# Weight signs on ScalarE, weight differences on GpSimd, and a new order of all engines, in a recurrent attention and feed-forward kernel

## The chip, the core and the metric

The kernel runs on one core of a Trainium2 chip. The time is device microseconds of one execution of the whole program, and the median of several runs is given. A profile of one execution stands beside it. The engines are TensorE (PE; its weight loads are PEld), VectorE (DVE), ScalarE (ACT), GpSimd (POOL) and SyncE (SP), which issues every DMA.

## The reference

```python
q, k, v, alpha: (4, 8, 768, 48)         # batch, heads, positions, head size
for t in range(S):                      # S = 768
    state = alpha[:, :, t, :, None] * state + einsum('bhd,bhe->bhde', k[:, :, t], v[:, :, t])
    y[:, :, t] = einsum('bhd,bhde->bhe', q[:, :, t], state)
x = y.transpose(0, 2, 1, 3).reshape(3072, 384)
h = x @ w_in                            # (384, 2048)
g = h * clip(h + 3, 0, 6) / 6
out = g @ w_out                         # (2048, 384)
```

The two weights come to the kernel as 64-bit floats, everything else as 32-bit floats.

## The kernel before

**Tiles.** The 3072 tokens are 24 chunks of 128 (j = 0 to 23), six to a batch. Two chunks are a group (g = 0 to 11). A chunk goes through the recurrence in blocked form and gives 128 columns of x; a group goes through the feed-forward part.

**Recurrence, chunk j.** `la`, `lk`, `lq`, `lv` load alpha, k, q, v. For j under 6, `ta`, `tk`, `tq` transpose on TensorE into one of four PSUM banks and `ca` copies alpha out on ScalarE; from j = 6 on, these transposes are stream transposes of VectorE (line 286) out of tiles `aq`, `kq`, `qq`, two of each. Those tiles have a strip of padding that GpSimd sets to one with a memset (line 257) when a tile is first used (j = 6 and 7). `r` and `p` are the two decay scans on VectorE (lines 309 and 320), `k` and `q` scale k and q (line 332), `sc` and `m` are scores and mask, `qa` copies q beside the masked scores (ScalarE), `kb`/`ck` (or `kt`, `kw`, `kr` through DRAM) turn k round, `u` is the state update on TensorE, `sm` adds it up on VectorE (`sm.j.0` the half state), `st` decays it on GpSimd (line 409), `sv` places it (ScalarE), `ya` and `yb` are the output of both half blocks, `cy` copies it into x (ScalarE).

**Weights.** They come in 16 slices of 128x768 64-bit words (`w.i`, 768 KB each): 0 to 7 are `w_in`, 8 to 15 `w_out`. A slice lands in one of three raw buffers (two more lie in the tile of hidden values). `d1` rounds the low words and `d2` takes the magnitude of the high words (ScalarE), `d3` clips and shifts them (VectorE), `d4` adds the low words (GpSimd, line 217). The sign has two forms. In the usual form the third instruction of `d3`, a mask and an or (line 210), puts the sign bits back. For the slices in `BY_HALVES` the step `dx` (`sign`, ScalarE, line 191) writes the sign into the low words instead, and `d3` has two instructions (lines 203 and 205).

**Feed-forward.** Groups 0 and 1 use plain products, `f.g.i` (`fa` and `fb` a chunk at a time) with relu `fr` (ScalarE) and product `fg` (VectorE), and chunks 0 and 1 use `b` for the second weight, with the copy `bo` and the store `so`. From group 2 on, the first weight is used in 20 fast products `M.g.i` of sums of x (`xc`) and sums of weights (`y`, 25 of them, VectorE, made once); `n` copies products out (ScalarE), `o` combines them (VectorE), `e` and `h` are relu and product. From group 1 on, the second weight is used in seven fast products `P.g.i` of 128x192 outputs. They need sums of hidden values (`s`, VectorE) and four differences of the weight's quarters, `x.0` to `x.3`, each 128x1536, made once: `x.0` and `x.2` are read by P.g.4 and P.g.2, `x.1` by P.g.3, `x.3` by P.g.6; `x.1` overwrites a quarter that `b.1.0`, `b.1.1`, `b.0.0` and `b.0.1` read. `K` copies partial outputs (ScalarE), `G.g.i` finishes an output quarter (VectorE; `G.g.3` a copy on ScalarE), `O.g.i` stores it.

**Order.** Nothing is scheduled at run time. A string of 1788 words is the program's order: each word is a step and its numbers (`fa.2.0` is weight slice 2 into bank 0), and each engine does its own steps in the order of the string, waiting by semaphore for what a step reads. `z.m.n` are n matmuls of the identity with no use for their result. SyncE's queue is in the same order: a DMA that waits holds up those behind it. In before, the differences are VectorE's:

```python
    def minus(out, in0, in1):
        nc.vector.tensor_tensor(out=out, in0=in0, in1=in1, op=ALU.subtract)

    def combine_w2(i):
        minus(*[(t[3], b[1, 1], b[0, 1]), (t[1], b[0, 1], b[0, 0]), (t[2], b[1, 1], t[1]),
                (t[4], b[1, 0], t[2])][i])
```

Of the kernel before, what the change touches and what calls it, by code (L numbers as in the profile page):

```python
# [17 lines left out]
def kernel(  # L18
# [32 lines left out]
    nc = tc.nc  # L51
# [124 lines left out]
    BY_HALVES = {0, 1, 2, 4}  # L176
# [573 lines left out]
    with tc.manual_schedule():  # L750
        run("""z.0.5 z.0.3 z.0.1 z.0.8 qa.0.0 w.0 d2.0 d3.0 la.0 ta.0.0 ca.0 r.0 lk.0 tk.0.1 k.0
               z.0.2 p.0 la.1 ta.1.2 lq.0 tq.0.3 ca.1 r.1 lk.1 lv.0.0 sv.0.0 d1.0 kb.0.0 ck.0 z.0.2
               u.0.2.1 sm.0.0 sv.0.1 q.0 qa.0.1 tk.1.0 k.1 p.1 z.0.2 sc.0.2.3 m.0 la.2 ta.2.0 ca.2
               dx.0 w.2 d2.2 kb.1.0 ck.1 lq.1 r.2 sm.0.1 st.1 tq.1.2 q.1 d3.2 z.0.3 d1.2 dx.2 lv.1.1
               u.1.3.1 sv.1.0 sm.1.0 p.2 sm.1.1 sc.1.0.2 m.1 ya.0.3 yb.0 cy.0 lq.2 w.1 d1.1 tq.2.1
               q.2 d4.2 lk.2 tk.2.3 k.2 fa.2.0 d4.0 st.2 sc.2.0.2 d2.1 d3.1 m.2 dx.1 d4.1 qa.1.1
               lk.3 la.3 ta.3.1 ca.3 la.4 fa.0.1 sv.1.1 w.3 r.3 ta.4.3 ca.4 r.4 tk.3.1 k.3 kb.2.0
               qa.1.0 d2.3 ya.1.2 yb.1 cy.1 fa.1.2 lq.3 ck.2 d1.3 p.3 d3.3 lv.2.2 u.2.3.2 sm.2.0
               d4.3 fb.2 tq.3.1 q.3 fb.1 qa.2.0 sm.2.1 sv.2.0 st.3 fr.0.2.0 fg.0.2 lk.4 tk.4.0
               sv.2.1 w.5 d2.5 k.4 d3.5 d1.5 qa.3.0 d4.5 qa.2.1 sc.3.1.3 m.3 w.6 d2.6 d1.6 d3.6 d4.6  # L760
               lv.3.0 lq.4 w.7 kb.3.2 fb.0 f.0.3.3 kb.4.0 ya.2.1 ck.3 u.3.3.2 sm.3.0 fr.0.3.1 fg.0.3
               fr.0.1.0 fg.0.1 qa.3.1 sv.3.0 sm.3.1 p.4 d2.7 sv.3.1 d1.7 d3.7 d4.7 f.0.5.0 fr.0.5.1
               fr.0.0.0 fg.0.5 fg.0.0 tq.4.3 ck.4 la.5 ta.5.2 f.0.6.3 ca.5 w.4 d2.4 ya.3.0 yb.3 cy.3
               fr.0.6.1 yb.2 cy.2 w.9 d2.9 q.4 qa.4.1 d1.4 d1.9 dx.4 la.6 w.8 d3.4 r.5 lk.5 w.10
               d3.9 p.5 ca.6 fg.0.6 d4.9 w.12 lq.5 lv.4.1 d2.8 d3.8 f.0.7.2 d1.8 st.4 d4.8 d4.4 w.11
               fr.0.7.0 fg.0.7 f.1.7.0 fr.1.7.1 fg.1.7 sc.4.0.2 m.4 f.1.1.1 fr.1.1.0 fg.1.1 f.1.3.3
               fr.1.3.1 d2.10 d1.10 tk.5.3 f.1.0.2 d2.12 d3.10 d4.10 w.13 fg.1.3 fr.1.0.0 fg.1.0 k.5
               d3.12 lq.6 f.1.6.0 f.1.2.1 u.4.1.0 sm.4.0 d1.12 d4.12 sv.4.0 qa.4.0 ya.4.2 fr.1.6.1
               fg.1.6 w.15 tq.5.3 fa.4.3 sv.4.1 d2.11 kb.5.1 d2.13 fr.1.2.0 f.1.4.2 fr.1.4.1 d1.11
               sm.4.1 q.5 r.6 d3.11 d3.13 fg.1.4 d4.11 lv.5.0 lk.6 tq.6 p.6 d2.15 d3.15 fg.1.2 d1.13  # L770
               d4.13 sc.5.0.3 yb.4 f.1.5.0 fr.1.5.1 fg.1.5 tk.6 m.5 b.1.0.2 fb.4 b.1.1 d1.15 d4.15
               st.5 y.5 w.14 la.7 lk.7 cy.4 d2.14 qa.5.1 ck.5 b.0.0.1 fr.0.4.0 d3.14 k.6 q.6 ca.7
               fg.0.4 d1.14 d4.14 x.0 y.1 y.10 b.0.1 y.0 y.2 u.5.2 P.1.0.0 K.1.0 qa.5.0 sv.5.0
# [159 lines left out]
```

## Time and profile before

| | us |
|---|---|
| median of 3 runs | 536.4 (536.31 to 536.47) |
| the profiled execution's own time | 536.33 |
| its span, first to last instruction | 534.5 |
| TensorE busy | 524.2 |
| VectorE busy | 477.1 |
| ScalarE busy | 257.6 |
| GpSimd busy | 50.4 |
| `d3` third instruction (line 210), mean of one | 0.96 |
| sign on ScalarE (line 191), mean of one | 1.94 |
| a difference of 128x1536 on VectorE (line 647) | 1.74 to 1.75 |

The page's busy times are of one execution, and a matmul counts as busy until its modelled end, so neighbours overlap. A row of the groups gives line, engine, operation, written and read tiles with their shapes and the count, then the group's busy time and the mean of one in ns, then the engine's idle time just before them and who ended it. A row of the timeline gives start, length, engine, line and operation, and in brackets the idle time before it and its releaser. A row of the chain of work that ended last gives start, length, engine, tile, line and count.

Busy time counts a tail that overlaps the next instruction. Where an engine is never idle, a step costs the distance from its start to the next start, and this is shorter: 1.35 us for the two instructions of `d3` in the halves form and 2.09 for the three of the usual form, 1.67 for a sign, 1.67 for a difference on VectorE, 1.54 for a mask step, 1.34 for `r`, 1.14 for `p`, 0.6 for `q`, `y` and most other steps of 128x512.

### The profile page before, as it was taken

The page shows a single profiled execution, that of the slowest core. Times are in us where ns is not written, and L with a number is a line of the kernel's source. Part 1 is how long each engine was busy: PE and PEld are TensorE (multiplying, and loading weights), DVE is VectorE, ACT ScalarE, POOL GpSimd, SP SyncE. Part 2 cuts the span into 40 slices and gives each one's busy share as a digit, 9 for nine tenths or more (in the row PEclk, how much of TensorE's full clock was granted, in tenths as well). Part 3 has the DMA queues.
Part 4 walks back from the last instruction along what each step waited for, and adds up shares of the span by engine and source line. Part 5 has one row for each costly group of instructions (what it writes and reads, how often), then busy time and mean ns, then how long its engine had stood idle before and what let it go on. Part 6 is the DMA issues. An engine that isn't in the chain of part 4 may idle for free.

```text
span 534.5 us, 15145 instructions
## 1 busy us (share of the span) xinstructions
PE 524.2 (98%) x6306; PEld 498.9 (93%) x6306; DVE 477.1 (89%) x849; ACT 257.6 (48%) x503; POOL 50.4 (9%) x71
## 2 busy tenths in 40 slices
PE   7799999999999999999999999999999999999997
PEld 7698886789999999999999999999999999999996
DVE  6999989999999899998999999999999898586381
ACT  3889864212653553543644434642633544553330
POOL 5333435100000000000010000000000000000000
PEclk9999999999999999999999999999999999999999
DMA  9998877006615155254354455055364042100001
GB/s 174 215 255 256 208 220 164 7 2 158 149 32 121 28 132 130 50 136 101 82 109 113 95 124 139 20 129 122 81 144 97 18 97 48 36 3 1 29 1 44
DMA packets 124100, 54.40 MB, mean 102 GB/s; under 512 B 83328, under 2 KB 116864, under 8 KB 124032
## 3 DMA queue, kind: packets, MB, share of 16 engines
q1 hardware_dynamic: 124032, 53.44, 43.0%
q8 instruction: 49, 0.80, 0.7%
q14 instruction: 19, 0.16, 0.1%
HBM read 44.50 MB, written 8.91 MB: 100 GB/s over the span
## 4 chain that ended last, share of the span: by engine, by line
PE 88%; DVE 6%; POOL 2%; ACT 1%; DMA 1%; issue 0%; SPq 0%; DVEq 0%; POOLq 0%
PE m_ps L703 34%; PE m_ps L600 34%; PE m_ps L478 6%; PE t_ps L455 4%; PE t_ps L346 2%; PE t_ps L429 2%; PE m_ps L489 2%; DMA v<-in_v_dram 1%; PE m_ps L516 1%; DVE rings L647 1%; PE t_ps L282 1%; DVE raw L537 1%; ACT raw L191 1%; DVE g_sb L647 1%; DVE w L537 1%; POOL v L96 1%
## 5 line engine op out<-in xcount | busy, mean ns | idle before, releaser
L606 ACT COPY g_sb<-m_ps 128x512 f32<-128x512 f32 x110 | 63.7, 584 | 124.1 <-PE m_ps L600 101.3
L703 PE MATMUL m_ps<-w,g_sb 128*128 128x192 f32 x704 | 121.7, 327 | 0.0
L703 PEld LDWEIGHTS m_ps<-w,g_sb 128*128 128x128 f32 x704 | 113.7, 190 | 0.4
L703 PE MATMUL m_ps<-rings,g_sb 128*128 128x192 f32 x528 | 91.5, 326 | 0.0
L703 PEld LDWEIGHTS m_ps<-rings,g_sb 128*128 128x128 f32 x528 | 85.4, 190 | 0.1
L600 PE MATMUL m_ps<-xc,w 128*128 128x128 f32 x640 | 82.7, 277 | 0.3 <-DVE w L541 0.3
L600 PEld LDWEIGHTS m_ps<-xc,w 128*128 128x128 f32 x640 | 77.5, 192 | 1.5 <-issue 0.5
L494 ACT ACTIVATE r<-g_sb,half 128x512 f32<-128x512 f32 x80 | 57.0, 722 | 31.5 <-DVE g_sb L541 12.4
L498 DVE SCALAR_TENSOR_TENSOR g_sb<-r,g_sb 128x512 f32<-128x512 f32 x80 | 53.7, 682 | 6.8 <-ACT r L494 5.4
L600 PE MATMUL m_ps<-xT,raw 128*128 128x128 f32 x400 | 52.5, 277 | 0.0
L600 PEld LDWEIGHTS m_ps<-xT,raw 128*128 128x128 f32 x400 | 48.6, 192 | 0.6
L409 POOL TENSOR_TENSOR st<-sm,R 128x192 f32<-128x192 f32 x20 | 12.9, 643 | 353.7 <-DVE sm L439 295.7
L647 DVE TENSOR_TENSOR g_sb<-g_sb 128x512 f32<-128x512 f32 (+1 forms) x55 | 42.1, 793 | 1.3 <-PE m_ps L703 1.1
L600 PE MATMUL m_ps<-xT,w 128*128 128x128 f32 x320 | 42.0, 276 | 0.0
L600 PEld LDWEIGHTS m_ps<-xT,w 128*128 128x128 f32 x320 | 39.3, 192 | 0.1
L366 ACT COPY A<-q 48x256 f32<-48x256 f32 x88 | 35.5, 404 | 5.0 <-DVE q L332 3.7
L356 DVE TENSOR_TENSOR A<-t_ps,mask 64x256 f32<-64x256 f32 x96 | 36.0, 413 | 0.4
L478 PE MATMUL m_ps<-xT,w 128*128 128x256 f32 x144 | 32.8, 382 | 0.0
L600 PE MATMUL m_ps<-xc,raw 128*128 128x128 f32 x240 | 31.8, 276 | 0.0
L478 PEld LDWEIGHTS m_ps<-xT,w 128*128 128x128 f32 x144 | 26.7, 190 | 3.6
L309 DVE TENSOR_TENSOR_SCAN R<-t,ones 128x516 f32<-128x516 f32 x24 | 29.6, 1233 | 0.5 <-ACT t L300 0.4
L600 PEld LDWEIGHTS m_ps<-xc,raw 128*128 128x128 f32 x240 | 29.6, 192 | 0.1
(104 smaller groups left out, 730.3 us busy)
## 6 DMA issues: line engine op xcount, KB each, us to landing
raw<-in_moe_w_out_dram SPq DMA_DIRECT2D x8, 768.0 KB, 5.3
raw<-in_moe_w_in_dram SPq DMA_DIRECT2D x6, 768.0 KB, 7.1
v<-in_v_dram SPq DMA_DIRECT2D x48, 96.0 KB, 3.0
out_dram<-oh SPq DMA_DIRECT2D x44, 96.0 KB, 1.7
far<-kq SPq DMA_DIRECT2D x64, 64.0 KB, 2.2
kb<-far SPq DMA_DIRECT2D x64, 64.0 KB, 2.1
aq<-in_alpha_dram SPq DMA_DIRECT2D x36, 96.0 KB, 2.4
qq<-in_q_dram SPq DMA_DIRECT2D x36, 96.0 KB, 2.5
```

The source lines that it names most:

```text
L309: nc.vector.tensor_tensor_scan(out=reverse(R, n - 1, n), data0=reverse(ax, n, n), data1=reverse(ones, n, n), initial=0.0, op0=ALU.mult, op ...
L356: nc.vector.tensor_tensor(out=to[:, a], in0=sc[a][half], in1=mask[half, half].unsqueeze(1).to_broadcast([HB, NP, HB]), op=ALU.mult)
L366: nc.scalar.copy(out=to[:, a], in_=Q_t[j][64 * a : 64 * a + D, :, half])
L409: nc.gpsimd.tensor_tensor(out=st, in0=sm, in1=R_t[j][:, :, 0:1].to_broadcast([C, NP, D]), op=ALU.mult)
L455: nc.tensor.matmul(y_of(j, (i + 1) // 2, p)[:, HB * b : HB * b + HB], vb[:, p, e : e + 32], A_t[j][:, b, 2 * p + a], start=(b == 0 and i = ...
L478: nc.tensor.matmul(h[:, f], w1[:, kk, o : o + C], xT_t[g][:, kk], start=(kk == 0), stop=(kk == KT - 1))
L494: nc.scalar.activation(out=to, in_=h, func=AF.Relu, bias=half, scale=1.0 / 6.0)
L498: nc.vector.scalar_tensor_tensor(out=to, in0=r, scalar=1.0, in1=h, op0=ALU.min, op1=ALU.mult)
L600: nc.tensor.matmul(acc[g][i][:, f * C : (f + 1) * C], spots[w][:, f * C : (f + 1) * C], x_of(g, x), start=(first and f == 0), stop=last, s ...
L606: nc.scalar.copy(out=slots[z], in_=acc[g][i])
L647: nc.vector.tensor_tensor(out=out, in0=in0, in1=in1, op=ALU.subtract)
L703: nc.tensor.matmul(to[g], a, rhs[:, f], start=(first and f == 0), stop=(last and f == HF - 1), skip_group_check=True)
```

## The change

The second weight's slices 8 to 15 take the halves form: eight more `dx` steps on ScalarE, and for these slices two instructions of `d3` in place of three. The four differences `x` go from VectorE to GpSimd. The string is a new one of 1796 words; the steps are otherwise the same, and TensorE does the same 6306 instructions. The line numbers behind the differences move by three (L647 for GpSimd's differences becomes L650).

```diff
-    BY_HALVES = {0, 1, 2, 4}
+    BY_HALVES = {0, 1, 2, 4, *range(8, 16)}
...
+    def less(out, in0, in1):
+        nc.gpsimd.tensor_tensor(out=out, in0=in0, in1=in1, op=ALU.subtract)
+
     def combine_w2(i):
-        minus(*[(t[3], b[1, 1], b[0, 1]), (t[1], b[0, 1], b[0, 0]), (t[2], b[1, 1], t[1]),
+        less(*[(t[3], b[1, 1], b[0, 1]), (t[1], b[0, 1], b[0, 0]), (t[2], b[1, 1], t[1]),
                 (t[4], b[1, 0], t[2])][i])
...
-  run("""z.0.5 z.0.3 z.0.1 z.0.8 qa.0.0 w.0 d2.0 d3.0 la.0 ta.0.0 ca.0 r.0 lk.0 tk.0.1 k.0
-      z.0.2 p.0 la.1 ta.1.2 lq.0 tq.0.3 ca.1 r.1 lk.1 lv.0.0 sv.0.0 d1.0 kb.0.0 ck.0 z.0.2
-      u.0.2.1 sm.0.0 sv.0.1 q.0 qa.0.1 tk.1.0 k.1 p.1 z.0.2 sc.0.2.3 m.0 la.2 ta.2.0 ca.2
-      dx.0 w.2 d2.2 kb.1.0 ck.1 lq.1 r.2 sm.0.1 st.1 tq.1.2 q.1 d3.2 z.0.3 d1.2 dx.2 lv.1.1
-      u.1.3.1 sv.1.0 sm.1.0 p.2 sm.1.1 sc.1.0.2 m.1 ya.0.3 yb.0 cy.0 lq.2 w.1 d1.1 tq.2.1
-      q.2 d4.2 lk.2 tk.2.3 k.2 fa.2.0 d4.0 st.2 sc.2.0.2 d2.1 d3.1 m.2 dx.1 d4.1 qa.1.1
-      lk.3 la.3 ta.3.1 ca.3 la.4 fa.0.1 sv.1.1 w.3 r.3 ta.4.3 ca.4 r.4 tk.3.1 k.3 kb.2.0
-      qa.1.0 d2.3 ya.1.2 yb.1 cy.1 fa.1.2 lq.3 ck.2 d1.3 p.3 d3.3 lv.2.2 u.2.3.2 sm.2.0
-      d4.3 fb.2 tq.3.1 q.3 fb.1 qa.2.0 sm.2.1 sv.2.0 st.3 fr.0.2.0 fg.0.2 lk.4 tk.4.0
-      sv.2.1 w.5 d2.5 k.4 d3.5 d1.5 qa.3.0 d4.5 qa.2.1 sc.3.1.3 m.3 w.6 d2.6 d1.6 d3.6 d4.6
-      lv.3.0 lq.4 w.7 kb.3.2 fb.0 f.0.3.3 kb.4.0 ya.2.1 ck.3 u.3.3.2 sm.3.0 fr.0.3.1 fg.0.3
...
-      st.5 y.5 w.14 la.7 lk.7 cy.4 d2.14 qa.5.1 ck.5 b.0.0.1 fr.0.4.0 d3.14 k.6 q.6 ca.7
-      fg.0.4 d1.14 d4.14 x.0 y.1 y.10 b.0.1 y.0 y.2 u.5.2 P.1.0.0 K.1.0 qa.5.0 sv.5.0
-      qa.6.1 P.1.1.3 b.0.2 b.1.2 kb.6.0 ya.5.3 y.6 s.1.0.0 sm.5.0 sv.5.1 G.1.0.0 tk.7
-      s.1.1.1 s.1.2.3 x.1 yb.5 cy.5 b.1.3 sc.6.1.2 lv.6.2 ck.6 u.6.3.0 s.1.3.2 x.2 P.1.2
-      b.0.3 K.1.1 y.7 s.1.4 s.1.5 y.11 y.3 r.7 xc.2.1 x.3 y.4 y.8 xc.2.3 k.7 xc.2.0 xc.2.4
-      y.9 y.12 y.16 y.13 y.15 P.1.3.3 K.1.2 P.1.4 bo.1 P.1.5 xc.2.5 G.1.1.1 P.1.6 y.14 y.17
-      y.19 xc.2.6 sm.6.0 G.1.2.2 y.20 M.2.0.2 lv.12.1 la.8 O.1.1 O.1.0 ca.8 y.18 y.21 y.23
...
-      s.11.1.14 s.11.3.10 P.11.3.2 K.11.0 s.11.2.11 o.11.2.1 o.11.3.1 P.11.2 K.11.2
-      e.11.2.0 h.11.2 s.11.4 e.11.3.1 h.11.3 P.11.1.0 s.11.5 G.11.0.1 O.11.0 O.10.3 K.11.1
-      P.11.4 G.11.1.2 P.11.5 G.11.2.1 O.11.2 P.11.6 G.11.3.0 O.11.3 O.9.2 O.11.1""")
+  run("""z.0.3 z.0.2 z.0.8 qa.0.0 w.0 d2.0 d1.0 la.0 ta.0.0 ca.0 z.0.2 lk.0 tk.0.1 d3.0 r.0
+      k.0 p.0 dx.0 la.1 ta.1.2 ca.1 r.1 kb.0.3 ck.0 lq.0 z.0.2 tq.0.0 lv.0.0 u.0.1.2 sm.0.0
+      sv.0.1 z.0.5 q.0 qa.0.1 sc.0.1.3 sm.0.1 p.1 m.0 w.2 d2.2 z.0.3 lk.1 tk.1.0 k.1 lq.1
+      d1.2 dx.2 tq.1.2 q.1 z.0.1 kb.1.1 sc.1.0.3 d3.2 m.1 qa.1.0 ck.1 w.1 d2.1 d3.1 la.2
+      sv.0.0 ya.0.2 yb.0 cy.0 d4.0 lv.1.1 st.1 sv.1.0 ta.2.1 ca.2 d1.1 dx.1 d4.2 fa.2.0
+      u.1.2.0 fa.0.1 r.2 sm.1.0 p.2 sm.1.1 lk.2 tk.2.3 k.2 lq.2 tq.2.1 q.2 la.3 qa.1.1
+      sv.1.1 ta.3.2 ca.3 ya.1.0 yb.1 cy.1 d4.1 st.2 w.5 d2.5 r.3 qa.2.1 d1.5 d3.5 d4.5
+      sc.2.1.3 m.2 kb.2.2 fa.1.2 fb.1 w.7 d2.7 ck.2 w.6 lv.2.2 d1.7 p.3 d2.6 d3.6 d1.6 d4.6
+      fb.2 fr.0.2.0 fb.0 fg.0.2 f.0.5.3 fr.0.0.1 qa.2.0 sv.2.0 u.2.0.2 sm.2.0 sv.2.1 lk.3
+      lq.3 fr.0.5.0 tq.3.1 q.3 qa.3.0 tk.3.3 d3.7 d4.7 ya.2.0 yb.2 la.5 ta.5.1 cy.2 f.0.6.0
...
+      k.6 y.2 d4.13 b.0.1 fa.4.2 fb.4 fr.0.4.1 w.15 d2.15 sv.4.0 st.5 d1.15 dx.15 qa.4.1
+      fg.0.4 d3.15 ca.7 r.8 y.0 m.4 d4.15 y.3 f.1.5.3 fr.1.5.0 fg.1.5 qa.5.0 kb.6.3 f.1.3.2
+      kb.5.2 ck.5 b.1.2 lv.5.0 lq.7 u.5.0 sc.5.1.2 f.1.4.3 fr.1.4.1 x.0 x.1 x.2 fr.1.3.0
+      m.5 b.1.3 b.0.2 tk.7 fg.1.3 P.1.0.2 b.0.3 lq.6 qa.4.0 tq.6 lq.8 sv.5.0 ck.6 sv.4.1
+      qa.5.1 sm.5.0 sv.5.1 K.1.0 ya.5.1 ya.4.2 yb.5 yb.4 bo.1 so.1 cy.5 fg.1.4 y.8 s.1.1.1
+      s.1.0.0 y.5 P.1.3.3 s.1.4 s.1.3.2 y.6 s.1.2.3 q.6 y.7 y.11 y.9 r.7 cy.4 xc.2.1 xc.2.2
+      y.10 y.4 y.15 y.12 y.16 y.13 y.17 xc.2.3 xc.2.4 P.1.2 tq.7 sc.6.0.3 la.10 lk.8 lv.7.0
+      lk.9 tk.8 u.6.1.2 qa.6.1 tq.8 K.1.1 P.1.4 K.1.2 G.1.1.0 bo.0 x.3 y.19 P.1.1.0 s.1.5
+      P.1.6 G.1.3.1 P.1.5 G.1.0.2 y.18 y.14 xc.2.5 y.21 xc.2.6 k.7 y.20 xc.2.10 sm.6.0
+      xc.2.0 xc.2.7 M.2.0.1 n.2.0.8 G.1.2.3 sm.6.1 y.23 xc.2.8 xc.2.9 m.6 p.7 k.8 q.7 y.22
...
+      o.11.2.1 P.11.3.3 O.10.3 K.11.0 s.11.3.9 P.11.2 e.11.2.1 h.11.2 o.11.3.0 o.11.3.1
+      K.11.2 e.11.3.0 s.11.4 h.11.3 P.11.1.2 s.11.5 G.11.0.3 O.11.0 K.11.1 P.11.4 G.11.1.2
+      P.11.5 P.11.6 O.11.1 O.9.1 G.11.2.0 O.11.2 G.11.3.3 O.11.3""")
```

## The prediction

> **What bounds it now.** The page comes first, then busy time by stage, then the chain.
>
> ```profile
> PE 524.2 (98%) x6306; PEld 498.9 (93%) x6306; DVE 477.1 (89%) x849; ACT 257.6 (48%) x503; POOL 50.4 (9%) x71
> ```
> ```profile
> 0.00:40.08 40.08, 33.86 (x548) 1.00 1.11 215
> 40.08:125.60 85.52, 85.52 (x838) 1.00 0.53 142
> 125.60:510.60 385.00, 384.71 (x4797) 1.00 0.37 86
> 510.60:534.50 23.90, 20.13 (x129) 1.00 0.08 25
> ```
> ```profile
> 149.23 2.60 PE m_ps L703 x16
> 159.04 2.68 PE m_ps L600 x24
> 58.20 5.38 PE m_ps L478 x24
> ```
>
> The stage rows give bounds, length, TensorE's busy time and instructions, granted clock, DMA share and GB/s. TensorE has next to no idle time from 40 to 510 us, at full clock. It is late only in the first 40 us and in the last 4. Busy is not full pace, so I price TensorE's steps at their undisturbed pace, start to start: P 2.60, M 0.89 (2.68 for three), f 2.59, b 2.58, fa/fb 1.34, short steps 0.44 to 0.56, z 0.22 a matmul. All steps of before come to 511.7 us. A step's *lateness* is its start less the priced steps before it. It is 1.5 us at TensorE's first instruction, 11.8 at 40.08, 13.3 at M.2.0 (125.70) and 19.0 at the end of P.11.6 (530.73). The last 5.7 are mostly some 30 pauses of 0.10 us, spread evenly and the same beside every step; I leave them. So taking 12.7 us off VectorE is worth nothing in itself: VectorE must lie ahead of a wait of TensorE.
>
> **Ramp.** Why is TensorE late there?
>
> ```profile
> 13.79 0.36 DVE L437 COPY s<-t_ps 128x192 f32<-128x192 f32 x1 [0.57 <-PE t_ps L429]
> 21.00 0.69 DVE L205 TENSOR_SCALAR w<-w 128x768 uint32<-128x768 uint32 x1
> 22.68 3.88 POOL L217 TENSOR_TENSOR w<-w,raw 128x768 int32<-128x768 int32 x2 [2.26 <-ACT raw L191]
> 24.80 1.60 PE L489 MATMUL m_ps<-xT,w 128*128 128x128 f32 x12 [0.20 <-POOL w L217]
> ```
>
> VectorE works almost without a gap from 13.8 us; d3.2 ends at 21.7, ScalarE's sign dx.2 at 22.6, GpSimd's d4.2 at 24.7, and only then fa.2 starts. I follow the new order with before's durations and landings (a weight slice 2.2 us behind the transfer before it, k or q 1.2, v 1.3).
> - Four idle matmuls fewer stand ahead of ta.0: it starts when alpha has landed (6.8 us, not 7.5); r.0 at 8.25, not 8.71; p.0 ends 11.3.
> - v.0 is sent before k.1: landed 11.7, so u.0 ends 12.3 and half-state, q.0, p.1, m.0 end 12.9, 13.6, 15.0, 16.5 (m.0 was 17.9).
> - w.2 now lands at 13.9 (was 16.1), k.1 behind it at 15.1 (was 11.7), q.1 16.3. tk.1 and tq.1 end by 16.9, so k.1 and q.1 follow m.0 unhindered, 17.7; d3.2 ends 19.05 (r.2, 1.34 us, moved behind it). ScalarE has dx.2 done at 18.1. d4.2 ends 21.1, cy.0 20.3: fa.2 starts 21.2 instead of 24.8.
> - Behind: VectorE has d3.1, r.2, sm.1.0, p.2, sm.1.1 up to 25.0, k.2 and q.2 up to 26.2, ScalarE dx.1 up to 24.0, qa.1 and sv.1 up to 25.5. yb.1 ends 26.7, then sc.2, kb.2, fa.1, three fb without a wait: f.0.5 at 33.1 with 24.7 us priced before it: lateness 8.4 against 11.8.
>
> The pass allows nothing for hand-offs, so I take 3.0 of the 3.4. Bounds: 1.7 from VectorE's queue alone (before, k.2 has 17.8 us of VectorE work up to its end and 15.3 of TensorE work ahead of its reader sc.2: 2.5 short; after, q.2 is 0.85 short), and 4.0.
>
> **Signs.** Eight slices lose the 0.96 us mask (L210) but take the dearer halves form: 1.35 instead of 2.09 us, 5.9 us less VectorE. ScalarE gains 8 x 1.67 = 13.4 us, GpSimd 8 x 0.4 = 3 (L217 1.86 to 1.93 instead of 1.47 to 1.61).
>
> ```profile
> L191 ACT ACTIVATE raw<-raw 128x768 f16<-128x768 int32 x3 | 5.8, 1942 | 0.1
> L217 POOL TENSOR_TENSOR w<-raw 128x768 int32<-128x768 int32 x11 | 17.7, 1608 | 32.4 <-DVE raw L210 15.2 <-ACT raw L186 6.7 <-issue 4.3
> L217 POOL TENSOR_TENSOR w<-w,raw 128x768 int32<-128x768 int32 x3 | 5.7, 1929 | 3.0 <-ACT raw L191 3.0
> L409 POOL TENSOR_TENSOR st<-sm,R 128x192 f32<-128x192 f32 x20 | 12.9, 643 | 353.7 <-DVE sm L439 295.7 <-ACT v L419 47.1 <-ACT A L366 10.9
> ```
>
> Queued behind the signs on ScalarE are copies that release banks (fr, cy, ck). With its work summed in the new order, ScalarE ends cy.3 at 49.9 us, 1.5 before TensorE wants f.1.1, and ck.5 at 85.4, 2 before u.5: I cost the signs at nothing, and at up to 1 us if that cover is gone because a slice lands late. GpSimd's 0.4 us more per slice releases the slices' buffers later; w.15 still lands near 77, 2 us before ScalarE asks for it.
>
> **Differences on GpSimd.** VectorE loses 4 x 1.67 = 6.7 us. GpSimd has no row of 128x1536: the two forms of L217 scale to 3.2 and 3.9 us, L409 to 5.1, the fastest additions (1.47) to 2.9. I take 3.5, between the rows nearest in size. What is queued behind them is the point. The padding memset of lq.6 stands behind x.2 on GpSimd, and VectorE's tq.6 waits for it with everything behind: sm.5, s.1.0 (read by P.1.3) and the weight sums y that M.2.0 reads. ScalarE's fr.0.4 waits for fb.4 (78.8 at lateness 8.4), then come d2.15, sv.4, d1.15 and dx.15 (0.58 + 0.82 + 0.74 + 0.82 + 1.67), up to 83.4. d4.15 ends 85.4, x.2 at 96.1 (three of 3.5, 0.2 between), the memset at 96.5. VectorE has ended m.5, tk.7 and fg.1.3 behind sc.5 (88.6 + 1.54 + 0.95 + 0.6) at 91.7 and idles 4.8 us. Then tq.6, sm.5, fg.1.4 to 98.3, while x.3 runs from 96.5 to 100.0. Does VectorE run beside it?
>
> ```profile
> 92.40 1.69 POOL L217 TENSOR_TENSOR w<-raw 128x768 int32<-128x768 int32 x1 [3.75 <-DVE raw L210]
> 92.69 1.96 DVE L332 TENSOR_TENSOR q<-q,P 128x512 f32<-128x512 f32 x1
> ```
>
> That product of two SBUF tiles takes 0.75 us on average, here 1.96, ending half a microsecond after GpSimd's addition does. So y.8, also of two SBUF tiles, starts at 100.0. From there to y.20 lie 22.6 us of VectorE work: M.2.0 can start at 122.6. TensorE is there at 121.2 (112.0 priced, lateness 9.2 with the pauses): 1.4 us of stall. P.1.3 (about 104) still has s.1.0 in time (101.8), and the state product st.7 behind x.3 is wanted only by ya.7, 20 us on. Lateness at M.2.0 is 10.6 against 13.3: 2.7 gained by then, ramp included. At 2.9 us each y.20 ends 120.2 and the gain is 4.1; at 5.1 P.1.3 stalls too, y.20 ends 129.0, lateness is 17.0 and 3.7 is lost.
>
> The Trainium skill speaks against this move: "GPSIMD Engine Reference", section 4.1, gives two-input elementwise work to VectorE as about twice as fast, and section 3.1's 4.5 us for 2048 elements would make 3.4 us here (an estimate), a stall of 1.0. "SBUF — State Buffer", section "Who interferes with whom", says that VectorE with two SBUF inputs and a reading GpSimd exclude each other for a whole instruction; the 1.96 us row agrees. Without that rule y.8 would start at 98.3 and M.2.0 would not stall.
>
> **Other terms.** In TensorE's order a long step follows a short one (scores, update, attend) 32 times instead of 37, and a short one a long one 35 times instead of 36. Each switch costs about 0.1 us (M takes 0.98 before a short step), so the new order is priced at 511.2 instead of 511.7: -0.5, bounds 0 and -0.7. Behind M.2.0 the nearest VectorE need has 0.4 us of cover up to 160 us, 3 later: 0, bounds -0.5 and +1.5. The end:
>
> ```profile
> 528.61 3.79 SPq L724 DMA_DIRECT2D out_dram<-oh  x4
> 530.77 0.32 ACT L716 COPY oh<-m_ps 128x192 f32<-128x192 f32 x1 [10.08 <-PE m_ps L703]
> ```
>
> Three stores follow the last copy (531.09), 0.43 us each to issue, up to 532.40. In the new order O.11.1, O.9.1 and O.11.2 go out under P.11.6 and one is left: -0.9, bounds 0 and -1.3.
>
> **Sum.** The profiled execution took 536.33 (span 534.5 and 1.8 around it; the median is 536.4). -2.7 - 0.5 + 0 - 0.9 = -4.1: 532.2 us.
>
> **Rivals.**
> 1. The differences don't stall anything (2.9 us each, or no exclusion): -4.1 - 0.5 - 0.9 = -5.5, 530.8. For it: the fastest additions. Against: the mean rows.
> 2. The ramp gives nothing, since k.1 behind a 768 KB slice reaches VectorE late or ScalarE's queue holds fa.2: lateness stays 11.8 at 40 us, TensorE then covers the stall at M.2.0, and -0.5 - 0.9 is left: 534.9. Against it: k.1 has 1 us of cover and VectorE other work.
> 3. Slower: GpSimd's four differences at L409's rate, 5.1 us. TensorE waits at P.1.3 and M.2.0: +3.7 - 0.5 - 0.9 = +2.3, 538.6. M.2.0 moves by 4 us for each microsecond of the price, so all of the gain is gone at 4.5 us each, and the mechanism decides from there.
> 4. The change does less than it says: the built program has the eight signs on ScalarE and the four subtractions on GpSimd, so this is out.
>
> **Chances.** The forecast gets 0.47, rival 1 0.18, rival 2 0.15, rival 3 0.15, other stalls in the new order 0.05. A difference under 0.2% (1.1 us) is about what a measurement of this kernel can't tell from none. Faster is the sum of the first three less 0.02 (rival 2 lies near the bound): 0.78; within it 0.05; slower 0.17. Range: 530.2 is rival 1 with the ramp at its upper bound, 536.6 is rival 2 with the 1.5 us that may be lost behind M.2.0; beyond lies rival 3.
>
> **What would show it.** First fa (L489) near 21 us, not 24.8; TensorE busy for over 35 of the first 40 us. The subtractions on GpSimd (now near L650) 3.2 to 3.9 us; a gap on VectorE of 4 to 5 us before a stream transpose near 92 us; M.2.0 between 121 and 124 us; one store issue after the last copy. It is wrong if the GpSimd row is over 4.5 us, if fa starts after 23, or if waits on VectorE or ScalarE appear in TensorE's list between 130 and 510.

## The result and the profile after

The changed kernel takes 542.1 us (median of 4 runs, 540.06 to 543.31) against 536.4 us before (536.31 to 536.69): ratio 1.0097, interval 1.0084 to 1.011. The forecast was 532.2. The profiled execution took 543.31 us, with a span of 541.5; before, 536.33 and 534.5. The term by term comparison below is made between these two executions; the changed kernel's is the slowest of its four.

The first part of the page after, busy time of each engine, and the granted clock in 40 slices:

```profile
PE 524.4 (97%) x6306; PEld 499.3 (92%) x6306; DVE 478.4 (88%) x837; ACT 272.4 (50%) x511; POOL 71.3 (13%) x75
PEclk9999999799999999999999999999999999999999
```

VectorE lost 12.6 us of work and is busy for 478.4 us, 1.3 more than before. Something gave its instructions back the time that was taken from it. One slice of the clock row shows 7.

The stages after, at the bounds that the prediction used (length; busy time of PE, PEld, DVE, ACT and POOL with their instructions; clock; DMA share; GB/s), and three short stretches in the bad one:

```profile
0.00:40.08 40.08, 34.10 (x548) 30.83 (x552) 34.76 (x60) 30.85 (x48) 19.52 (x27) 1.00 1.02 218
40.08:125.60 85.52, 77.20 (x794) 61.26 (x783) 78.16 (x110) 57.49 (x84) 39.99 (x30) 0.96 0.63 158
125.60:510.60 385.00, 385.00 (x4791) 379.40 (x4790) 348.41 (x644) 176.62 (x366) 11.79 (x18) 1.00 0.35 81
```
```profile
91.00:98.00 7.00, 3.34 (x34) 1.96 (x35) 6.92 (x8) 1.23 (x3) 6.75 (x5) 1.00 0.00 0
98.00:101.00 3.00, 0.74 (x38) 0.60 (x32) 2.97 (x3) 0.00 (x0) 2.92 (x2) 0.60 0.00 0
101.00:106.00 5.00, 5.00 (x13) 4.05 (x14) 2.36 (x5) 0.00 (x0) 4.82 (x4) 0.55 0.00 0
```

Before, TensorE was busy for 85.52 of the 85.52 us of the second stage; after, for 77.20. From 91 to 101 us it is busy for 4 us of 10, VectorE and GpSimd nearly all the time, and from 98 to 106 us the granted clock is 0.60 and 0.55. By *lateness* (a step's start less the priced steps before it) the account is: 10.5 us at f.0.5 (forecast 8.4), 14.4 when b.1.2 ends at 93.7 us, 22.9 behind f.1.4, 23.1 at M.2.0, which starts at 135.15, and 27.5 at the end of P.11.6. Waits that stand in the text without a timeline row are counted like this, start to start over the priced steps; the gaps that the profile shows are 0.1 to 0.3 us shorter.

What were VectorE, GpSimd and TensorE doing there? The timelines of the changed kernel, VectorE first, then GpSimd, then TensorE:

```profile
89.81 2.68 DVE L309 TENSOR_TENSOR_SCAN R<-t,ones 128x516 f32<-128x516 f32 x1
92.62 3.64 DVE L537 TENSOR_TENSOR raw<-w 128x512 f32<-128x512 f32 x1
96.18 1.52 DVE L356 TENSOR_TENSOR A<-t_ps,mask 64x256 f32<-64x256 f32 x4
97.74 2.36 DVE L539 TENSOR_TENSOR raw<-w 128x512 f32<-128x512 f32 x1
100.13 0.69 DVE L498 SCALAR_TENSOR_TENSOR g_sb<-r,m_ps 128x512 f32<-128x512 f32 x1
```
```profile
89.55 1.86 POOL L217 TENSOR_TENSOR w<-w,raw 128x768 int32<-128x768 int32 x1 [1.90 <-ACT raw L191]
91.87 3.84 POOL L650 TENSOR_TENSOR rings<-w 128x1536 f32<-128x1536 f32 x1
95.79 3.76 POOL L650 TENSOR_TENSOR w<-w 128x1536 f32<-128x1536 f32 x1
```
```profile
97.47 0.57 PE L429 MATMUL t_ps<-v,kb 64*64 64x48 f32 x13 [3.66 <-issue]
100.87 5.10 PE L478 MATMUL m_ps<-xT,w 128*128 128x256 f32 x12 [2.26 <-DVE g_sb L498]
```

Read them against each other. VectorE's scan r.8 takes 2.68 us instead of 1.23 and ends 1.1 us behind GpSimd's addition d4.15; its weight sum y.0 takes 3.64 instead of 0.69, beside the difference x.0 (91.87 to 95.71); y.3 takes 2.36 instead of 0.68, beside x.1. Each has two SBUF inputs. In before y.0 and y.3 stood beside no instruction of GpSimd:

```profile
99.22 0.69 DVE L537 TENSOR_TENSOR raw<-w 128x512 f32<-128x512 f32 x1
111.76 0.68 DVE L539 TENSOR_TENSOR raw<-w 128x512 f32<-128x512 f32 x1
```

Behind y.0 stands the mask step m.4, for whose bank u.5.0 waits 3.66 us (the timeline calls it "issue"; the four instructions of m.4 run from 96.18 to 97.70, and u.5.0 starts when those that read its bank are through); behind y.3 stands fg.1.5, for whose bank f.1.4 waits 2.26. Then f.1.4 itself takes 4.94 us to the next step instead of 2.59, because the clock is down. 3.7 + 2.4 + 2.4 = 8.5 us, the step from 14.4 to 22.9.

Ramp and tail, in the timeline of the changed kernel:

```profile
22.84 1.58 PE L489 MATMUL m_ps<-xT,w 128*128 128x128 f32 x12 [0.75 <-ACT xT L464]
...
536.59 2.83 SPq L727 DMA_DIRECT2D out_dram<-oh  x2
538.74 0.32 ACT L719 COPY oh<-m_ps 128x192 f32<-128x192 f32 x1 [10.08 <-PE m_ps L706]
```

The first fa starts at 22.84 us (24.80 before; 21.2 forecast), and now waits for ScalarE's copy of x. One store follows the last copy, and the span ends 2.8 us after the last matmul, where it was 3.8.

An account of VectorE up to the end of y.20, which M.2.0 reads, puts it in one row. *Blocked* is the time above the median of its form, in instructions that began while GpSimd was executing; *idle* is the gaps; *work* is the rest. Kernels of the next section stand with it.

| kernel | y.20 ends | work | blocked | idle |
|---|---|---|---|---|
| before | 124.8 | 114.4 | 3.6 | 6.8 |
| changed | 134.5 | 107.2 | 15.2 | 12.1 |
| before, differences on GpSimd | 133.3 | 107.7 | 14.8 | 10.8 |
| before, signs on ScalarE | 130.9 | 107.4 | 2.1 | 21.4 |
| changed, differences on VectorE | 131.4 | 113.5 | 11.0 | 7.0 |
| changed, GpSimd's differences only write | 129.5 | 107.1 | 9.4 | 13.0 |
| the same, and the additions of slices 8 to 15 only write | 127.1 | 107.8 | 5.7 | 13.6 |

So the change takes 7.2 us of work from VectorE, as it was to, and gives it 11.6 us of blocking and 5.3 of waiting.

### The profile page after: what moved, and what is told of

The parts are those of the page before. It is cut to its first block, busy times and chain, and to the rows that moved or that the text cites. A ratio compares the mean times of both kernels' runs of the same rounds, so it can differ in the third digit from the quotient of the medians.

```text
span 541.5 us, 15118 instructions
## 1 busy us (share of the span) xinstructions
PE 524.4 (97%) x6306; PEld 499.3 (92%) x6306; DVE 478.4 (88%) x837; ACT 272.4 (50%) x511; POOL 71.3 (13%) x75
## 4 chain that ended last, share of the span: by engine, by line
PE 81%; DVE 7%; DMA 6%; ACT 4%; issue 1%; POOL 1%; SPq 0%; DVEq 0%
PE m_ps L706 37%; PE m_ps L600 34%; PE t_ps L455 4%; DMA aq<-in_alpha_dram 2%; DMA raw<-in_moe_w_in_dram 2%; PE t_ps L346 2%; PE t_ps L429 2%; DMA g_sb<-in_moe_w_in_dram 1%; PE m_ps L516 1%; DVE R L309 1%; PE m_ps L478 1%; DVE raw L537 1%; ACT w L196 1%; DVE k L332 1%; ACT raw L191 1%
## 5 line engine op out<-in xcount | busy, mean ns | idle before, releaser
L706 PEld LDWEIGHTS m_ps<-rings,g_sb 128*128 128x128 f32 x528 | 85.4, 190 | 0.1
L600 PE MATMUL m_ps<-xc,w 128*128 128x128 f32 x640 | 84.0, 277 | 0.0
L409 POOL TENSOR_TENSOR st<-sm,R 128x192 f32<-128x192 f32 x20 | 15.4, 768 | 326.4 <-DVE sm L439 221.9
L647 DVE TENSOR_TENSOR g_sb<-g_sb 128x512 f32<-128x512 f32 (+1 forms) x55 | 41.8, 789 | 1.8 <-PE m_ps L706 1.7
L600 PEld LDWEIGHTS m_ps<-xT,w 128*128 128x128 f32 x320 | 38.8, 192 | 0.1
L478 PE MATMUL m_ps<-xT,w 128*128 128x256 f32 x144 | 35.3, 399 | 2.8 <-DVE g_sb L498 2.8
L478 PEld LDWEIGHTS m_ps<-xT,w 128*128 128x128 f32 x144 | 28.3, 201 | 7.5 <-DVE g_sb L498 3.2
L309 DVE TENSOR_TENSOR_SCAN R<-t,ones 128x516 f32<-128x516 f32 x24 | 33.2, 1385 | 0.6 <-ACT t L300 0.6
L537 DVE TENSOR_TENSOR g_sb<-g_sb 128x512 f32<-128x512 f32 x40 | 27.7, 700 | 5.8 <-ACT g_sb L606 5.8
```

Of the source, the lines that this page charges most:

```text
L309: nc.vector.tensor_tensor_scan(out=reverse(R, n - 1, n), data0=reverse(ax, n, n), data1=reverse(ones, n, n), initial=0.0, op0=ALU.mult, op ...
L478: nc.tensor.matmul(h[:, f], w1[:, kk, o : o + C], xT_t[g][:, kk], start=(kk == 0), stop=(kk == KT - 1))
L537: eng.tensor_tensor(out=out, in0=in0, in1=in1, op=ALU.add if s1 > 0 else ALU.subtract)
L600: nc.tensor.matmul(acc[g][i][:, f * C : (f + 1) * C], spots[w][:, f * C : (f + 1) * C], x_of(g, x), start=(first and f == 0), stop=last, s ...
L706: nc.tensor.matmul(to[g], a, rhs[:, f], start=(first and f == 0), stop=(last and f == HF - 1), skip_group_check=True)
```

## The experiments

My theory was exclusion: GpSimd's instructions hold up VectorE's, which stand ahead of what TensorE waits for. The rivals were the signs' time on ScalarE, the new order by itself, and a clock that falls for reasons of its own.

**Each edit alone, in both orders.** Six kernels complete a table of two orders by two edits. The edits are single lines:

```diff
-        less(*[(t[3], b[1, 1], b[0, 1]), ...        # a_diff_vector, a_none
+        minus(*[(t[3], b[1, 1], b[0, 1]), ...
-    BY_HALVES = {0, 1, 2, 4, *range(8, 16)}         # a_no_signs, a_none: and dx.8 to dx.15 out of the string
+    BY_HALVES = {0, 1, 2, 4}
```

and the reverse in before's string, each new dx behind its d1 (b_diff_gpsimd, b_signs, b_both).

> The changed kernel with the four differences back on VectorE, in the same place of the new order; the signs stay on ScalarE. Theory (exclusion): GpSimd's differences and additions hold up VectorE's instructions with two SBUF inputs ahead of the mask step m.4 and the product fg.1.5, TensorE idles 6.1 us at u.5.0 and f.1.4, and its granted clock then falls and costs 2.4 more. Without the differences on GpSimd those 8.5 us go: 533.6, with VectorE's y.0 and y.3 at 0.69 us each and full clock from 91 to 106 us; the 5.0 us that x.0 to x.2 take on VectorE fill its idle time before tq.6. Rival (signs): the eight signs and the weight slices that they delay (d4.15 ended 6 us later than forecast) set the stalls, so the time stays at 540 or more. Rival (order): the new order does it whatever the engine, 540 or more as well.

> The changed kernel without the eight signs: slices 8 to 15 in the usual form with VectorE's third instruction, same order, differences on GpSimd. Theory (exclusion): VectorE gets 5.9 us more work and still stands behind GpSimd, 541 to 546. Rival (signs): ScalarE loses 13.4 us and the slices arrive earlier, the stalls between 75 and 101 us go, 534 or less.

> The kernel before, in its own order, with only the four differences on GpSimd. Theory (exclusion): VectorE saves 6.7 us but its sums y beside x.0 to x.3 take up to 3.6 us instead of 0.69; four differences block up to 14 us in all, and P.1.2, P.1.4 or M.2.0 come later: slower by 1 to 6 us. Rival (order): the differences are harmless where the order leaves room, within 1 us of the kernel before or faster.

> The kernel before, in its own order, with only the eight signs on ScalarE, each behind its d1. Theory (exclusion): signs alone cost TensorE little, 535.5 to 537.5. Rival (signs): 13.4 us more on ScalarE ahead of the relu and copy steps that release banks cost TensorE 3 us or more: 539 or more.

> The kernel before, in its own order, with both edits: the eight signs on ScalarE and the differences on GpSimd. Alone they cost 5.7 and 8.2 us there. If they add up: 550. If one hides in the other: 545. The new order's own worth is the distance from here to the 542.1 of the changed kernel.

> The changed kernel's order alone: differences on VectorE in their new place, slices 8 to 15 in the usual form. Known are 540.1 (signs only) and 547.8 (differences only) in this order, 536.5, 542.3, 544.8 and 551.6 (neither, signs, differences, both) in the old one. If the new order is what loses (rival), this is 541 or more. By the accounts of VectorE: 5.9 us of work more than the run with signs only, of which VectorE has idle time for 2.5: 543 to 546. If the order fits the two edits and only they lose, 537 or less.

| median, us (ratio to before) | neither | signs | differences | both |
|---|---|---|---|---|
| old order | 536.5 | 542.3 (1.0073 to 1.0116) | 544.8 (1.0137 to 1.0172) | 551.6 (1.0255 to 1.03) |
| new order | 545.0 (1.014 to 1.0173) | 540.1 (1.0046 to 1.0076) | 547.8 (1.0192 to 1.0231) | 542.1 (1.0084 to 1.011) |

No cell beats the kernel before. The differences on GpSimd cost time in every pairing: 8.3 and 9.3 us in the old order, 2.8 and 2.0 in the new one; the last of these compares two sets of four runs whose ranges touch (540.06 to 543.31 and 539.72 to 540.16). The signs cost 5.8 and 6.8 us in the old order and are worth 4.9 and 5.7 in the new. The new order costs 8.5 us without the edits, and is worth 9.5 with both: it is an order for these edits, and it repairs most of what they spoil, not all. The theory had b_signs at 536.5 and b_diff_gpsimd at no more than 542.5, and was wrong on both; in the old order the two costs add up. a_none lies where VectorE's account put it (543 to 546); a_no_signs, expected at 541 to 546, came out at 547.8. My expectation for a_diff_vector, 533.6, failed as well: the clock stayed at 1.00 and y.0 and y.3 took their 0.66 and 0.69 us, but VectorE then had the 6.7 us itself: TensorE waited 1.7 us at P.1.6 for x.3 on VectorE, and came to M.2.0 (131.59) with y.20 just done (131.44). Both rivals, "signs" and "order", had expected 540 or more. The account shows why neither is the whole: with the differences back, 11.0 us of blocking by GpSimd's additions of weight slices are still there.

The old order shows the same lock at another place. In b_diff_gpsimd three weight sums of two SBUF inputs take 3.90 to 3.92 us each beside x.1 to x.3 (from 98.45 to 110.0 us). The half state sm.5.0 behind them in VectorE's queue starts at 111.17 instead of 101.62, ScalarE copies it, and the attend step ya.5 waits 6.15 us for that copy; TensorE's granted clock is 0.50 from 110.5 to 117.2 us, and the b step (8 matmuls) behind takes 4.91 us to the next step instead of 2.77. 6.2 and 2.1 are the 8.3 that this cell costs. In b_both four such sums are held and ya.5 waits 8.74 us.

**Signs in the old order.** The timeline of ScalarE in b_signs, and of TensorE beside it:

```profile
72.71 1.93 ACT L191 ACTIVATE raw<-raw 128x768 f16<-128x768 int32 x1
74.66 0.71 ACT L419 COPY v<-st 48x192 f32<-48x192 f32 x2
75.38 0.83 ACT L366 COPY A<-q 48x256 f32<-48x256 f32 x2
```
```profile
75.84 0.86 PE L455 MATMUL t_ps<-A,v 128*32 128x64 f32 x32 [1.53 <-ACT A L366]
```

The copies of state and q stand behind dx.12 in ScalarE's queue, and ya.4.2 waits for them. A kernel with short signs asks whether it is this time or something else in the halves form:

```diff
-        nc.scalar.activation(out=halves[:, :, :, 1], in_=hi.bitcast(I32), func=AF.Copy, scale=2.0**-64)
+        part = slice(0, 1 if i >= NW1 else None), slice(0, 96 if i >= NW1 else None)
+        nc.scalar.activation(out=halves[:, *part, 1], in_=hi.bitcast(I32)[:, *part], func=AF.Copy, scale=2.0**-64)
```

> The kernel before with the eight signs on ScalarE, as in the run that took 542.3, but each covers only 96 of the 768 columns (the signs of the others are left out), so that a sign takes about 0.3 us of ScalarE instead of 1.7; VectorE's shorter form and GpSimd's longer addition stay. If ScalarE's time in its queue, ahead of the state copies, relus and roundings, is what cost the 5.7 us: 535.5 to 537. If it is the longer additions on GpSimd or the added hand-off, it stays at 540 or more.

It took 536.55 us (ratio 0.9985 to 1.0003). So ScalarE's time in its queue is the price of the signs, and the 7.0 us less work on VectorE are worth nothing where VectorE isn't late.

**GpSimd that writes and doesn't read.** Memsets of the same length stand in for the differences, and in the second kernel for the additions of slices 8 to 15 too. These kernels leave out what those instructions read and compute; order, engines and GpSimd's time stay as they are.

```diff
     def less(out, in0, in1):
-        nc.gpsimd.tensor_tensor(out=out, in0=in0, in1=in1, op=ALU.subtract)
+        for n in (HF, HF, HF // 2):
+            nc.gpsimd.memset(out[:, 0:n], 1.0)
...
         dst, lo, hi = slice_of(i)                    # add_low, a_write_all only
+        if i >= NW1:
+            for to in (lo, dst, dst[:, 0:1]):
+                nc.gpsimd.memset(to.bitcast(FP), 1.0)
+            return
```

> The changed kernel, same order and same engine for everything, but each difference on GpSimd is replaced by three memsets of its target (8, 8 and 4 of the 8 rows of 192), so that GpSimd writes for about as long (128x1024 takes 0.96 us in the trace, so about 3.6 us) and reads no SBUF. The second weight's differences are left out by this. Theory (exclusion by GpSimd's reads): y.0 and y.3 take 0.69 us, the wait at u.5.0 falls from 3.7 to 0.7 us and that at f.1.4 from 2.4 to 0.7, the clock stays full (2.4): 535, the waits of 3.1 us between 75 and 88 us stay. Rival (the order, or GpSimd's time itself: the weights being ready late): nothing changes, 541 or more.

> As the one before, and the eight additions of slices 8 to 15 on GpSimd are replaced by memsets of the low words, of the weight and of half of it (about 1.8 us together), behind the same signs and shifts; the second weight's values are left out. Theory (exclusion by reads, for all slow VectorE instructions): the waits of 3.1 us between 75 and 88 us go as well: 532. If GpSimd's writes hold VectorE's fast one-input instructions (lines 203 and 205, 0.56 us) as its reads hold the two-input ones, these stay near 2 us and the time near 535.

The first took 538.09 us (ratio 1.0012 to 1.0032), 4.0 less than the changed kernel. Its timelines of VectorE and GpSimd:

```profile
91.39 2.06 DVE L537 TENSOR_TENSOR raw<-w 128x512 f32<-128x512 f32 x1
94.92 0.69 DVE L539 TENSOR_TENSOR raw<-w 128x512 f32<-128x512 f32 x1
104.49 1.29 DVE L286 STREAM_TRANSPOSE q<-qq 128x512 f32<-128x512 f32 x1 [3.23 <-POOL qq L257]
```
```profile
90.41 2.48 POOL L217 TENSOR_TENSOR w<-w,raw 128x768 int32<-128x768 int32 x1 [2.39 <-ACT raw L191]
93.34 3.62 POOL L651 MEMSET rings<- 128x1536 f32 x3
```

y.3 takes 0.69 us beside memsets that keep GpSimd just as busy (3.62 us); y.0 takes 2.06, since here it falls beside d4.15, which still reads. The waits at u.5.0 and f.1.4 are 0.65 and 0.73 us, the clock 1.00: 7.1 us less in that place. Not all arrives: TensorE now waits 1.0 us at P.1.6 for VectorE and comes to M.2.0 with y.20 just done. The theory is confirmed for the wait, and the expected 535 was 3 us too low, because I had not counted that VectorE's queue sets M.2.0 next. The second took 537.0 us (0.9988 to 1.0013; its profiled execution 535.81), not 532: the wait at fa.4.2 fell from 1.6 to 0.55 us, but VectorE's one-input instructions of lines 203 and 205 were held by writes too (one of 0.56 us took 1.12 beside a memset), and P.1.6 waits 1.9 us for VectorE. Some 1.3 us of that miss go with the clock: of its ten runs four have a mean granted clock of 1.000 and take 535.4 to 535.8 us, the profiled one among them, and six have 0.996 to 0.997 and take 536.9 to 538.0.

**The blocked instructions moved.** In the changed kernel's string r.8, y.0 and y.3 go from ahead of m.4 and fg.1.5 to behind s.1.0, and lq.6 ahead of x.0:

```diff
-  fg.0.4 d3.15 ca.7 r.8 y.0 m.4 d4.15 y.3 f.1.5.3 ... fr.1.4.1 x.0 x.1 x.2 ... b.0.3 lq.6 ... fg.1.4 y.8 s.1.1.1 s.1.0.0 y.5
+  fg.0.4 d3.15 ca.7 m.4 d4.15 f.1.5.3 ... fr.1.4.1 lq.6 x.0 x.1 x.2 ... b.0.3 ... fg.1.4 s.1.1.1 s.1.0.0 y.0 y.3 r.8 y.8 y.5
```

> The changed kernel with r.8, y.0 and y.3 (all of two SBUF inputs) taken from ahead of m.4 and fg.1.5 and put behind s.1.0, y.8 behind them, and the load lq.6 with its padding memset ahead of x.0. Theory (exclusion): m.4 and fg.1.5 no longer stand behind blocked instructions; the waits at u.5.0 and f.1.4 go (6.1 us) and the clock stays full (2.4), but the two-input work of VectorE now waits for x.2 and x.3 later, and M.2.0 still waits for y.20: no better than the kernel whose GpSimd read nothing (538.1), so 538 to 540. Rival (these instructions are not what holds m.4 and fg.1.5): 542.

It took 541.5 us (1.0076 to 1.0103). VectorE's and TensorE's timelines, and the clock:

```profile
102.84 4.61 DVE L667 TENSOR_TENSOR g_sb<-g_sb 128x512 f32<-128x512 f32 x2
```
```profile
114.28 2.84 PE L706 MATMUL m_ps<-rings,g_sb 128*128 128x192 f32 x16 [1.51 <-DVE g_sb L647]
126.41 4.45 PE L706 MATMUL m_ps<-rings,g_sb 128*128 128x192 f32 x16 [2.81 <-DVE oh L722]
```
```profile
126.00:131.00 5.00, 4.59 (x18) 4.62 (x19) 5.00 (x12) 0.10 (x1) 0.00 (x0) 0.66 0.01 3
```

The waits at u.5.0 and f.1.4 are gone altogether, so these instructions were what held m.4 and fg.1.5. The time is not: now s.1.1 and s.1.0 are blocked by x.3 (4.61 us for 1.26), VectorE comes late to P.1.2 and to P.1.6, and the clock falls there. Moving the victims moves the wait. The measured time is nearer to the rival's 542 than to my 538 to 540; the rows decide for the mechanism.

**The clock.** Idle matmuls fill TensorE's gaps:

```diff
-  b.1.2 lv.5.0 lq.7 u.5.0 sc.5.1.2 f.1.4.3
+  b.1.2 lv.5.0 lq.7 z.6.17 u.5.0 sc.5.1.2 f.1.4.3               # a_filled
+  b.1.2 lv.5.0 lq.7 z.6.17 u.5.0 sc.5.1.2 z.6.10 f.1.4.3        # a_filled2
```

> The changed kernel with 17 idle matmuls (0.22 us each, 3.8 us) ahead of u.5.0, into the bank that ck.5 has released, so that TensorE is busy while it waits for the mask step m.4; nothing else. Theory (the clock falls because TensorE stood idle): f.1.4 takes 2.6 us again instead of 4.9, the granted clock stays at 1.00 from 98 to 106 us, 539.8. Rival (the clock has nothing to do with this gap): f.1.4 stays at 4.9 us, 542.

> The changed kernel with 17 idle matmuls ahead of u.5.0 and 10 (2.2 us) ahead of f.1.4, into columns that no step uses, so that TensorE stands still neither before u.5.0 nor before f.1.4. With the first 17 alone f.1.4 still took 4.25 us and the clock was 0.68 from 101 to 106 us. Theory (TensorE's idle time lowers its clock): f.1.4 takes 2.6 us and the clock is 1.00 from 98 to 106; the time is 2 us below the changed kernel's, unless VectorE's queue takes it back at M.2.0, where y.20 ended 0.6 us before TensorE came: so f.1.4 and the clock decide, and 540 to 542. Rival: f.1.4 stays above 4 us.

The windows 98 to 101 and 101 to 106 us, of a_filled and then of a_filled2:

```profile
98.00:101.00 3.00, 0.86 (x46) 0.72 (x42) 2.97 (x3) 0.00 (x0) 2.92 (x2) 0.97 0.00 0
101.00:106.00 5.00, 4.95 (x15) 3.93 (x16) 2.53 (x5) 0.49 (x1) 4.82 (x4) 0.68 0.02 3
```
```profile
98.00:101.00 3.00, 3.00 (x66) 2.93 (x67) 2.94 (x3) 0.00 (x0) 2.92 (x2) 1.00 0.02 5
101.00:106.00 5.00, 5.00 (x24) 3.89 (x23) 3.38 (x7) 1.80 (x4) 4.82 (x4) 1.00 0.00 0
```

With one gap filled the clock still fell, after the other gap of 2.2 us, and the time (543.0, 540.28 to 544.6) told nothing. With both filled it stayed at 1.00, f.1.4 took 2.65 us, and the kernel 541.4 (541.22 to 541.46). Against the profiled execution of the changed kernel M.2.0 came 1.85 us earlier, and the span is 1.8 shorter; the four runs lie within 0.24 us, those of the changed kernel within 3.3. So TensorE's standing still lowers the clock here; that is worth some 1.9 us in an execution where it falls, and the waits themselves are the larger part.

**The ramp and the tail alone.** In before: the tail's two stores moved; then the changed kernel's first 96 words ahead of the rest; then two repairs at the seam.

```diff
-  G.11.1.2 P.11.5 G.11.2.1 O.11.2 P.11.6 G.11.3.0 O.11.3 O.9.2 O.11.1
+  G.11.1.2 O.11.1 O.9.2 P.11.5 G.11.2.1 O.11.2 P.11.6 G.11.3.0 O.11.3            # all three
-  sc.2.0.2 m.2 lk.3 la.4 w.3 r.3 ... p.3 d3.3 lv.2.2 u.2.3.2 sm.2.0 d4.3 fb.2 tq.3.1 q.3 fb.1 qa.2.0 sm.2.1
+  sc.2.0.2 r.3 m.2 lk.3 la.4 w.3 ... p.3 lv.2.2 u.2.3.2 sm.2.0 fb.2 tq.3.1 q.3 fb.1 qa.2.0 sm.2.1 d3.3 d4.3   # c_best
```

> The kernel before with one thing moved: the stores O.11.1 and O.9.2 go ahead of P.11.5 instead of behind O.11.3. The forecast priced this at 0.9 us, and in the changed kernel's trace the span ended 2.8 us after the last matmul instead of 3.8: 535.6. Rival: something else sets the end, 536.6.

> As the one before, and the first 96 words of the changed kernel's string (up to st.2) stand ahead of the rest of the words of before, in their old order: the new ramp alone, with no sign and no difference moved. The changed kernel's trace has TensorE 0.7 us earlier at its first fa and 1.3 us less late at f.0.5 than before: 534.6, where the forecast had 3.0 for this. Rival: VectorE's queue behind the ramp sets M.2.0 whatever the ramp does (y.20 ended 0.9 us ahead of M.2.0 in before), so nothing beyond 0.5 comes of it: 535.3 or more.

> The kernel before with the new ramp and the new tail (537.7 as first joined, where TensorE waited 0.8 us at sc.2, 0.5 at kb.2 and 1.9 at sc.3), with two repairs at the seam: r.3 ahead of m.2, and d3.3 and d4.3 behind sm.2.1, so that q.3 and sm.2.0, which sc.3 needs, don't stand behind the weight slice on VectorE. If the ramp's gain of about 1 us is real and was only lost at the seam: 534.7. If the later order can't use an earlier TensorE: 535.5, as with the tail alone.

The tail alone: 535.45 us (ratio 0.997 to 0.9988), 1.0 less than before, as forecast; it is the fastest version measured here. The ramp joined to the old order: 537.7, and repaired 537.55, so it loses 2.1 us against the tail alone, and the expected 534.7 was wrong. Repaired, sc.3 no longer waits, but f.0.3 (for d4.3, 0.8 us) and later steps do, and y.20 ends at 127.1 instead of 125.4. What this ramp gained early, the old order behind it did not keep.

## Why the prediction was wrong

- **Ramp, +2.1 at f.0.5.** Most loads landed as forecast (w.2 at 13.97, k.1 at 15.18), r.0 and p.0 too (8.23; 11.38). The first step that failed is r.1, which the pass took at 1.34 us:

```profile
11.29 2.81 DVE L309 TENSOR_TENSOR_SCAN R<-t,ones 128x516 f32<-128x516 f32 x1
```
```profile
10.13 2.88 POOL L217 TENSOR_TENSOR w<-w,raw 128x768 int32<-128x768 int32 x1 [2.37 <-ACT raw L191]
```

  GpSimd's d4.0 stands beside it; that it holds r.1 up is read from these rows, and no run took d4.0 away. The half state came at 14.56, not 12.9, and fa.2 started at 22.84, not 21.2 (24.80 before), when d4.2 (22.60; forecast 21.1) and cy.0 (22.70; forecast 20.3) were done. The bounds of 1.7 to 4.0 were too high: TensorE's gain by f.0.5 was 1.3. The prediction's own sign, TensorE busy for over 35 of the first 40 us, failed too (34.10).
- **Signs at nothing.** Right in the new order in that ScalarE's queue cost TensorE nothing that shows; but in the old order 5.8 us. What I left out is their longer addition on GpSimd: I priced it as 3 us on an engine with time to spare, and not as 1.86 to 2.17 us each in which VectorE may stand still.
- **75 to 91 us, +3.3 that no term allowed for.** k.5, which u.4 waits for, and fg.1.0, which fa.4.2 waits for, stand behind d3.12 and d3.14. (The profile puts the wait of fa.4.2 down to GpSimd's d4.13, which ended last; in the kernel where that addition only writes, fa.4.2 starts 0.14 us behind fg.1.0.) VectorE's rows and GpSimd's:

```profile
73.81 2.10 DVE L205 TENSOR_SCALAR w<-w 128x768 uint32<-128x768 uint32 x1
76.42 1.89 DVE L203 TENSOR_SCALAR w<-w 128x768 f32<-128x768 f32 x1
```
```profile
73.44 2.04 POOL L217 TENSOR_TENSOR w<-w,g_sb 128x768 int32<-128x768 int32 x1 [6.31 <-DMA aq<-in_alpha_dram]
76.04 1.86 POOL L217 TENSOR_TENSOR w<-w,raw 128x768 int32<-128x768 int32 x1 [0.55 <-ACT raw L186]
```

  These have one SBUF input and take 0.56 us undisturbed. I had used the rule only for two inputs. The Trainium skill, "SBUF — State Buffer", section "Who interferes with whom", also names `tensor_scalar` in its fast form as taking the shared port; these rows agree, and with that half of the rule the 1.10 us row of this form at 26.02 in before (beside an addition that ended at 26.56) would have read as a warning.
- **Differences on GpSimd.** Their price was right: 3.44 to 3.84 us against 3.5. The idle time of VectorE behind the padding memset, 4.8 us in the forecast, did not come: in the changed kernel the memset was done at 103.78, and VectorE was held up by ScalarE's relu (3.92 us, ahead of fg.1.3) and began tq.6 at 108.21, 0.2 us behind that product. Where GpSimd only wrote, VectorE did wait for the memset, 3.2 us. The step that failed is "y.8 only": the forecast put one VectorE instruction beside x.3 and none beside x.0 to x.2 and d4.15. Since everything ran some 6 us later than forecast (d4.15 ended at 91.41, not 85.4), r.8, y.0 and y.3 met them, ahead of m.4 and fg.1.5: +6.1 and the clock's 2.4. The forecast stall of 1.4 at M.2.0 did not come, because TensorE was later still.
- **Tail.** -0.9 forecast, -1.0 measured. Behind M.2.0 TensorE lost 4.3 us to pauses, not 5.7.

The sum: 532.2 + 2.1 (ramp) + 3.3 + 8.5 - 1.4 (no stall at M.2.0) - 1.4 (fewer pauses) gives 543.3, the profiled 543.31, which is the slowest of the four runs; the median is 1.2 lower. Rival 3 had the sign and nearly the place, but its mechanism, a GpSimd price over 4.5 us, was not what happened; the cost lay in which VectorE instructions stand beside a GpSimd that reads, and not in how long it took: with memsets of the same length in place of the differences the kernel took 4.0 us less.

## What to carry to other kernels

Price work that is moved to GpSimd as a lock on VectorE: for as long as GpSimd reads, VectorE's two-input instructions and its fast one-input ones don't start (the latter were held here by memsets, which only write, as well), and what stands behind them in the queue waits too. Count it against the time that VectorE saves (here 7.2 us of work against 11.6 of blocking), and ask which VectorE instructions with a waiting reader lie beside each GpSimd instruction, also if all runs some microseconds later than planned. An order that is searched for a set of edits may be worth nothing without them: here it cost 8.5 us alone, and its ramp, joined to the old order, lost 2.1 against the tail alone; only the last stores, which touched nothing else, kept their gain.

## What the runs showed of the hardware

- In six kernels (before, changed, and the four of the first comparisons) some 50 VectorE instructions up to 140 us (47 to 54, by how finely their forms are told apart) took over 0.25 us more than the median of their form in before. All began while a GpSimd instruction was executing, and each ended 0.11 to 0.15 us short of that one's end plus its own usual duration (in one case, in a_diff_vector at 29.22, of the next GpSimd instruction's end): they did nothing until GpSimd was done. It holds the other way as well: d4.0 took 2.88 us instead of 1.86 where the scan p.0 ran beside it, and a difference takes 3.76 to 3.84 us where a held VectorE instruction was still finishing as it began (x.0 to x.2) and 3.44 with none beside (x.3).
- Cut into narrow windows, the granted clock of these traces is 1.00 or 0.50 in the stretches that count. It is 0.50 from 98.7 to 105.4 us in the changed kernel, from 110.5 to 117.2 in b_diff_gpsimd, and for 3.3 to 3.4 us from 100.9 in a_filled, from 126.3 in a_moved and from 77.1 in b_signs: one length, or twice that.
- TensorE's granted clock fell behind pauses of 3.7 and 2.3 us (changed), 2.8 us (a_moved), 2.2 us (a_filled), and in b_signs to 0.63 from 76 to 80 us behind one of 1.5; it did not behind one of 1.7 us between long steps (a_diff_vector, a_write_all). So the length of a pause alone doesn't decide. Ahead of the short ones that count stood steps of small matmuls (u and sc); whether these count as standing still was not tested. The Trainium skill, "TensorE: Matmul & The Clock Gate", Part 1, gives half rate after an idle window of about 3.4 us that runs freely. The half rate agrees (0.50 in the narrow windows), and so does the length of the stretches, but shorter pauses were enough. The spread of 3.3 us between the runs of the changed kernel, against 0.24 with the gaps filled, is the clock's only in part: the fastest run (540.06) has a mean granted clock of 0.997 and the other three 0.994, but these three take 541.11 to 543.31. What else sets them apart stays open.
